# Expert loop by pairs: where half of one tile's second layer, the slot tables and a weight refill stand

## The chip, the cores and the metric

The kernel runs on one core of a Trainium2 chip. The metric is the device time of one execution in microseconds (us); the time before is the median of three runs. The engines are TensorE (PE, with its weight loads as PEld), VectorE (DVE), ScalarE (ACT), GpSimd (POOL) and SyncE (SP, which here only starts transfers). Each works through a queue of its own in order, and waits on semaphores that the other engines count up.

## What is computed

A chunked attention (8 batches, 8 heads, 576 positions, chunks of 64) gives x, 4608 tokens of 512 numbers. Then a layer of 8 experts: each token gets one expert, by the largest of 8 router logits or, where a local gate is open, the expert of the token before it.

```
for b, s:
    fresh_e = argmax(x[b, s] @ w_gate)
    e = fresh_e if s == 0 or local_gate[b, s] < 0.5 else prev_e
    p = softmax(x[b, s] @ w_gate)
    out[b, s] = p[e] * (relu(x[b, s] @ w1[e]) @ w2[e])     # w1: 512 x 1024, w2: 1024 x 512
```

## The kernel before

**Stages.** Attention goes in 18 blocks of 256 tokens until about 174 us. Tokens are then sorted by expert into tiles of 128 slots, an expert's share rounded up to 64, so that a tile may hold the end of one expert and the beginning of the next (a mixed tile). Tiles 0 to 2 (`EARLY` = 3) always belong to expert 0 and come from the first half of the tokens; their two layers run in the drain of the attention, in an order written out by hand (`PAR["drain"]`: `x2` is tile 2's transposes and split, `m2` its layer 1, `h2` the transposes of h, `y2` the four quarters of its layer 2 and its output, `x3` and `x4` the same of tiles 3 and 4 as `x2`, `ex` steps of the table of experts, `sl` steps of a table of slots). From tile 3 on a loop takes two tiles at a time (`two`, sixteen pairs, a = 3, 5, ... 33), and the last tiles go one by one (`step`).

**Precision.** fp32 products are made of three passes with the operands split into a high and a low half: high x high, high x low, low x high. The high half is a cast on ACT, the low half a subtraction on DVE. That holds for x (`XP`), h (`HP`), and both weights (`w1h`, `w1l`, `w2h`, `w2l`, four chunks each).

**A pair.** In a uniform pair, where both tiles have one expert, layer 1 gives h already transposed, in eight blocks of 128 features, 256 tokens wide: 12 matmuls each (L992), two blocks to one PSUM bank of `TR` (three banks), which ACT and DVE then empty into h's halves, tile by tile (L999, L1000). Otherwise each tile has a layer 1 of its own (`up`, L684), and h is transposed afterwards (L650). `two(a)` runs: layer 1 for blocks 0 to 3; the rejoining of a mixed x; refill of w1 if tile a is the last of its expert; layer 2 of tile a-1 (`down`, L705, 24 matmuls of 512 columns in four quarters; not for the first pair); refill of w2 if tile a-1 was the last of its expert; three register loads for the next pair; layer 1 for blocks 4 to 7; transposes of the next two x tiles into `TR[1]` and `TR[2]` (`next_x`); the second refill of w1; layer 2 of tile a; the second refill of w2.

**Refill.** `refill(which, t)` stands under a conditional on a register that says whether tile t+1 has another expert. ACT casts four chunks of the loaded weights to the high half (`refill_hi`, L942), DVE subtracts four low halves (`refill_lo`, L948), and SP starts the load of the expert after that. An engine passes the conditional by a register load (L927), a compare-and-branch (L958) and a semaphore event, also where nothing is refilled; whoever reads the weights waits for that event. With `between` the refill of w2 is split: two chunks, then other work, then two chunks.

**Tables.** `slots` makes the gather and scatter indices. For tiles 9 and on it has four steps, `sl[0]` and `sl[1]` (one half of the tokens each, all on DVE, L597 to L601), `sl[2]` (36 matmuls) and `sl[3]`. The loop runs `sl[0:2]` after the first pair and `sl[2:4]` after the second.

**Tiles of this input.** Tile 5 is the last of expert 0, 8, 16, 19, 24, 25 and 32 those of the experts after it; 8, 19 and 32 are mixed. So tiles 5 and 6, 7 and 8, 19 and 20, 25 and 26, 31 and 32 are pairs without one expert, and the pairs that begin at tiles 9, 17, 25 and 33 refill w2 between their halves. Data of a few more names: `HB` and `MB` are the PSUM banks of `up` and of the mixed part, `YB` the two banks of layer 2's results, `hsb` h before its transposes.

Of the kernel before, what the change touches and what calls it, by code (L numbers as in the profile page):

```python
# [8 lines left out]
F32 = mybir.dt.float32  # L9
# [4 lines left out]
AF = mybir.ActivationFunctionType  # L14
# [40 lines left out]
    ),  # L55
    "p0": "AVPA",
    "p1": "PPPP",
# [11 lines left out]
def tile_attention_then_moe(ctx: ExitStack, tc, q, k, v, wg, wl, w1, w2, out):  # L69
# [432 lines left out]
    def run(fns):  # L502
        for fn in fns:
            fn()
# [218 lines left out]
    def new_y():  # L723
        return ps_o.tile([P, C], F32, name="y", tag="o")
# [31 lines left out]
    def x_atoms(t, ps=None):  # L756
        return hilo_atoms(lambda n: xgs[t][:, P * n:P * n + P], *x_of(t), ps)

    def h_of(t, g):
        return [HP[t % 3][g][:, a] for a in range(2)]  # L760

    def h_atoms(t, g, ps=None):
        return hilo_atoms(lambda n: hsb[:, 512 * g + P * n:512 * g + P * n + P], *h_of(t, g), ps)
# [32 lines left out]
        return atoms  # L796

    def early_m2(t):
        y = new_y()
        return [lambda c=c: mm2(0, y, c) for c in range(4)] + [lambda: emit_y(t, y, prc[t])]  # L800

# [154 lines left out]
    def refill(which, t, between=None):  # L956
        if between is None:
            with tc.If(reg(0, t, 1, [ET.Activation, ET.DVE, ET.SP]) != 0):  # L958
                refill_hi(which)
                refill_lo(which, t)  # L960
            return
        with tc.If(reg(0, t, 1, [ET.Activation]) != 0):
            refill_hi(which)
        with tc.If(reg(0, t, 1, [ET.DVE, ET.SP]) != 0):
            refill_lo(which, t, (0, 1))
        between()
        with tc.If(reg(0, t, 1, [ET.DVE, ET.SP]) != 0):
            refill_lo(which, t, (2, 3))
# [16 lines left out]
               lambda: (mm1_lower(pairx[:, 0], HB), mm1_upper(fullx, MB), relu_mixed(hsb, HB, MB)))  # L985

    def up_pair(a, f0):
        for f in range(f0, f0 + 4):
            hb = TR[f // 2 % 3]
            for c in range(4):  # L990
                for n, (x, w) in enumerate(PASSES):
                    nc.tensor.matmul(hb[:, 256 * (f % 2):256 * (f % 2) + 256], W1[w][c][:, P * f:P * f + P],  # L992
                                     XP[:, x, c].rearrange("p s t -> p (s t)"),
                                     start=(c == 0 and n == 0), stop=(c == 3 and n == 2))
            if f % 2:
                for n in range(2):
                    ps = hb.rearrange("p (f s t) -> p f s t", f=2, s=2)[:, :, n]
                    hi, lo = (z[:, f % 4 - 1:f % 4 + 1] for z in h_of(a + n, f // 4))
                    nc.scalar.activation(hi, ps, AF.Relu)  # L999
                    V.scalar_tensor_tensor(lo, ps, 0.0, hi.bitcast(F32), ALU.max, ALU.subtract)  # L1000

    def down(t, cs=range(4), shared=False):
        y, pr = YB[:, t % 2], prc[t]
        ysb = pc.tile([P, C], F32, name="ysb") if cs[-1] == 3 else None

        def plain():
            for c in cs:
                mm2(t, y, c)
            if cs[-1] == 3 and shared:
                V.tensor_scalar(ysb[:, 0:256], y[:, 0:256], pr, None, ALU.mult)  # L1010
                nc.scalar.mul(ysb[:, 256:C], y[:, 256:C], pr)
            elif cs[-1] == 3:
                V.tensor_scalar(ysb, y, pr, None, ALU.mult)  # L1013

        def both():
            for c in cs:
                mm2_lower([pair01[:, g] for g in range(2)], y, c)
            if cs[-1] == 3:
                mm2_upper(full01, MB)
                y_mixed(ysb, y, MB, pr)  # L1020

        either(mix[t], plain, both)
        if cs[-1] == 3:
            scatter(t, ysb)
# [19 lines left out]
    def two(a, uni):  # L1044
        pr = get_prob(a)
        run(pr[:2])
        with tc.If(nc.snap(uni, engines=list(MAN)) != 0) as cmp:
            up_pair(a, 0)
        with cmp.Else():
            up(a)  # L1050
        rejoin_x(a + 1)
        refill(0, a)
        run(pr[2:])
        if a > EARLY:
            down(a - 1)
        refill(1, a - 1)
        more = uniform(a + 2) if a + 2 in PAIRS else mix_of(a + 2)
        pr = get_prob(a + 1)
        run(pr[:2])

        def next_x():
            for n in range(1 + (a + 2 in PAIRS)):
                run(x_atoms(a + 2 + n, TR[1 + n]))

        with tc.If(uni != 0) as cmp:
            up_pair(a, 4)
            next_x()
        with cmp.Else():
            for g in range(2):
                run(h_atoms(a, g, TR[g]))  # L1070
            rejoin_h(a)
            up(a + 1)
            next_x()
            for g in range(2):
                run(h_atoms(a + 1, g, (TR[0], MB)[g]))
        rejoin_x(a + 2)
        refill(0, a + 1)
        run(pr[2:])
        down(a)
        refill(1, a)  # L1080
        rejoin_h(a + 1)
        return more
# [47 lines left out]
    def valid(t):  # L1130
        return reg(2, t, 1, [ET.PE, ET.Activation, ET.DVE, ET.Pool, ET.SP]) if t >= TMIN else None

    mix, ok = {}, {t: None for t in range(TMIN)}
    oks, mixs = {}, {}
    with tc.manual_schedule(engines=MAN | {ET.SP, ET.Pool}):
        HP += [[pa2.tile([P, 2, 4, P], F32R, name=f"hq{n}", tag=tag, bufs=bufs) for n, (tag, bufs) in enumerate(two_of)]
               for two_of in ((("xs", 3), ("xs", 3)), (("xs", 3), ("pT", 2)))]
        pairx = pc.tile([P, 1, 4, P], F32R, name="pairx", bufs=1)
        pair01 = pa2.tile([P, 2, 4, P], F32R, name="pair0", tag="xT", bufs=1)
        fullx, *full01 = [pc.tile([P, 4, HT], F32, name=f"full{n}", bufs=1) for n in "x01"]  # L1140
        TR += [trp() for _ in range(3)]
        HB = new_h()
        MB = ps_l.tile([P, 512], F32, name="m", tag="lg")
        YB = ps_o.tile([P, 2, C], F32, name="y", tag="o")
        for t in (EARLY + 2, EARLY + 3):
            gather_full(t)
        uni = uniform(EARLY)
        rejoin_x(EARLY)
        refill(0, EARLY - 1)
        for a in PAIRS:  # L1150
            uni = two(a, uni)
            if 19 <= a < 24:
                for t in (a + 17, a + 18):
                    oks[t] = valid(t)
                    mixs[t] = mixed(t)
            n = a - EARLY
            run(sl[n:n + 2])
            if a + 5 <= TMIN:
                for t in (a + 4, a + 5):
                    gather_full(t)  # L1160
            if a in (TMIN // 2 - 1, TMIN - 3):
                nc.gpsimd.drain()
        ok[TMIN] = oks[TMIN]
        for t in range(PAIRS[-1] + 2, TMIN + 3):
            step(t)
        with when(ok[TMIN + 2]):
            for t in range(TMIN + 3, NTILE + 1):
                step(t)
# [21 lines left out]
```

## Time and profile before

| | us |
|---|---|
| median of 3 runs | 673.73 (671.21 to 676.15) |
| the profiled execution | 672.63 |
| its span, first to last instruction | 670.8 |
| PE busy | 624.3 (93%) |
| DVE busy | 380.4 (57%) |
| ACT busy | 259.9 (39%) |
| POOL busy | 151.7 (23%) |
| mean granted PE clock | 0.987 of full speed |

The span is cut in 40 slices for the busy shares; PE's digit is 8 or 9 in all but the first and the last slice. The chain that ended last names PE for 1% of the span and little else, so it does not help here; the waits of PE and the timeline do. A row of the timeline gives start, duration, engine, line, operation, output<-inputs, shapes and count, and in brackets how long the engine was idle before it and what released it. A name such as DVEq L958 means an instruction of that engine's sequencer (a wait or a branch). Durations of matmuls are those of a pipeline, so the distance of starts tells their rate.

### The profile page before, as it was taken

How to read it: one execution, taken by the hardware profiler on the slowest of the kernel's cores; microseconds unless marked ns; L12 is line 12 of the kernel's file. 1: busy time of each engine (PE TensorE's matmuls, PEld its weight loads, DVE VectorE, ACT ScalarE, POOL GpSimd, SP SyncE). 2: the span in 40 equal slices, each digit the busy share in tenths (PEclk: the TensorE clock that was granted, in tenths of full speed). 3: DMA queues.
4: the chain of work that ended last, by engine and by line, in shares of the span. 5: the costliest groups of instructions: out<-in, count | busy, mean ns of one | idle time of the engine just before them, and what ended most of it. 6: DMA issues, size and time to landing. Idle time of an engine off the chain costs nothing. (4 is left out here: it accounts for less than half of the span.)

```text
span 670.8 us, 17087 instructions
## 1 busy us (share of the span) xinstructions
PE 624.3 (93%) x5904; PEld 520.8 (78%) x5904; DVE 380.4 (57%) x983; ACT 259.9 (39%) x469; POOL 151.7 (23%) x209
## 2 busy tenths in 40 slices
PE   4799998889998989999999999999998999999995
PEld 4678776767787868777989887788986988788883
DVE  2666766887785576476334365664377533377231
ACT  4577765665312144342112342532266121243120
POOL 4433333460051121111212022020211311111201
PEclk9999998898999999999999999999999999999998
DMA  9999999978622053254211155422257510154101
GB/s 249 263 253 282 263 276 273 240 212 256 208 72 105 22 172 106 87 174 141 67 50 38 47 175 170 159 85 103 66 177 268 183 52 34 49 176 141 67 20 36
DMA packets 102515, 97.57 MB, mean 145 GB/s; under 512 B 42256, under 2 KB 79120, under 8 KB 102352
## 3 DMA queue, kind: packets, MB, share of 16 engines
q1 hardware_dynamic: 96192, 75.69, 38.1%
q0 software_dynamic: 6160, 19.85, 9.0%
q8 instruction: 85, 1.39, 0.9%
q14 instruction: 78, 0.64, 0.3%
HBM read 76.48 MB, written 19.56 MB: 143 GB/s over the span
## 5 line engine op out<-in xcount | busy, mean ns | idle before, releaser
L992 PE MATMUL tr<-xp,w1h 128*128 128x256 f32 x704 | 130.9, 283 | 1.9 <-ACTq L958 1.7
L766 POOL DMA_INDIRECT out<-ysb,sidx x38 | 44.3, 1166 | 372.0 <-DVEq L958 219.9
L992 PEld LDWEIGHTS tr<-xp,w1h 128*128 128x128 f32 x704 | 111.0, 191 | 4.4 <-ACTq L958 1.9
L705 PE MATMUL y<-w2h,hq 128*128 128x512 f32 x320 | 105.3, 399 | 1.0 <-ACTq L980 1.0
L992 PE MATMUL tr<-xp,w1l 128*128 128x256 f32 x352 | 100.4, 285 | 2.8 <-DVE w1l L948 2.2
L705 PE MATMUL y<-w2h,hp 128*128 128x512 f32 x240 | 78.6, 396 | 0.6 <-ACT hp L652 0.3
L705 PEld LDWEIGHTS y<-w2h,hq 128*128 128x128 f32 x320 | 60.4, 189 | 15.0 <-issue 1.2
L992 PEld LDWEIGHTS tr<-xp,w1l 128*128 128x128 f32 x352 | 67.2, 191 | 5.2 <-DVE w1l L948 3.5
L705 PE MATMUL y<-w2l,hq 128*128 128x512 f32 x160 | 63.5, 397 | 0.0
L684 PE MATMUL h<-w1h,xp 128*128 128x512 f32 x208 | 60.7, 397 | 0.0
L999 ACT ACTIVATE hq<-tr 128x256 fp32r<-128x256 f32 x48 | 18.4, 384 | 104.3 <-PE tr L992 73.8
L705 PEld LDWEIGHTS y<-w2h,hp 128*128 128x128 f32 x240 | 44.9, 188 | 11.6 <-issue 1.4
L705 PE MATMUL y<-w2l,hp 128*128 128x512 f32 x120 | 46.8, 390 | 0.0
L1013 DVE TENSOR_SCALAR ysb<-y,ppr 128x512 f32<-128x512 f32 x31 | 23.3, 751 | 40.0 <-PE y L705 39.5
L656 POOL DMA_INDIRECT xg<-x_d,gidx x36 | 39.8, 1105 | 18.9 <-issue 8.5
L684 PEld LDWEIGHTS h<-w1h,xp 128*128 128x128 f32 x208 | 37.9, 188 | 7.3
L999 ACT ACTIVATE hp<-tr 128x256 fp32r<-128x256 f32 x40 | 15.3, 383 | 71.7 <-PE tr L992 60.2
L653 DVE TENSOR_TENSOR xp<-tr,xp 128x512 fp32r<-128x512 f32 x39 | 25.6, 687 | 24.5 <-ACT xp L652 17.9
L1000 DVE SCALAR_TENSOR_TENSOR hq<-tr,hq 128x256 fp32r<-128x256 f32 x48 | 20.4, 424 | 32.9 <-ACT hq L999 28.6
L751 ACT ACTIVATE hsb<-h 128x512 f32<-128x512 f32 x26 | 14.1, 596 | 63.8 <-PE h L684 49.6
L948 DVE TENSOR_TENSOR w1l<-raw,w1h 128x1024 fp32r<-128x1024 f32 x28 | 32.4, 1220 | 8.6 <-ACT w1h L942 4.2
L251 PE MATMUL o<-v,pT 64*64 64x65 f32 x1152 | 27.8, 227 | 8.7 <-DMA v<-in_v 4.2
(219 smaller groups left out, 1110.2 us busy)
## 6 DMA issues: line engine op xcount, KB each, us to landing
raw<-in_moe_w SPq DMA_DIRECT2D x72, 512.0 KB, 4.1
x_d<-xs SPq DMA_DIRECT2D x16, 521.0 KB, 5.7
v<-in_v SPq DMA_DIRECT2D x32, 256.0 KB, 6.6
qt<-in_q SPq DMA_DIRECT2D x15, 512.0 KB, 6.9
kt<-in_k SPq DMA_DIRECT2D x15, 512.0 KB, 5.8
x_d<-xs SPq DMA_DIRECT2D x8, 130.2 KB, 4.8
qt<-in_q SPq DMA_DIRECT2D x8, 128.0 KB
kt<-in_k SPq DMA_DIRECT2D x8, 128.0 KB, 4.4
```

The costliest lines, as they stand in the source:

```text
L251: nc.tensor.matmul(o[64 * cp:64 * cp + 64, cc, DV * h:DV * h + D + 1], pT[64 * cc:64 * cc + 64, 4 * j + h, 64 * cp:64 * cp + 64], vt[64 * ...
L653: lambda: V.tensor_tensor(lo, box["ps"], hi.bitcast(F32), ALU.subtract)]
L656: nc.gpsimd.indirect_dma_start(out=dst, out_offset=None, in_=src, in_offset=bass.IndirectOffsetOnAxis(ap=gidx[t].bitcast(U32), axis=0))
L684: nc.tensor.matmul(hs[:, j], xs[a][:, c], W1[w][c][:, 512 * j:512 * j + 512], start=(c == 0 and n == 0), stop=(c == 3 and n == 2))
L705: nc.tensor.matmul(y, h_of(t, f // 4)[a][:, f % 4], W2[w][c][:, f % 2, :], start=(f == 0 and n == 0), stop=(f == 7 and n == 2))
L751: nc.scalar.activation(hsb[:, 512 * j:512 * j + 512], hs[:, j], AF.Relu)
L766: nc.gpsimd.indirect_dma_start(out=out, out_offset=bass.IndirectOffsetOnAxis(ap=sidx[t].bitcast(U32), axis=0), in_=ysb, in_offset=None, bo ...
L948: V.tensor_tensor(lo[c], raw[c], hi[c].bitcast(F32), ALU.subtract)
L992: nc.tensor.matmul(hb[:, 256 * (f % 2):256 * (f % 2) + 256], W1[w][c][:, P * f:P * f + P], XP[:, x, c].rearrange("p s t -> p (s t)"), star ...
L999: nc.scalar.activation(hi, ps, AF.Relu)
L1000: V.scalar_tensor_tensor(lo, ps, 0.0, hi.bitcast(F32), ALU.max, ALU.subtract)
L1013: V.tensor_scalar(ysb, y, pr, None, ALU.mult)
```

## The change

Tile 2's layer 2 is cut: two quarters stay in the drain, the other two and the output come between the halves of the first pair's layer 1, where the later pairs have the layer 2 of the tile before. For this tile 2 writes into `YB`, which is made earlier, and h's buffers rotate by one so that tile 2 keeps its own. The first half of the table for tiles 9 and on moves from behind the first pair to a place in its middle, ahead of that layer 2. In a uniform pair's layer 1 two blocks now go together: first all passes with `w1h` (16 matmuls), then those with `w1l` (8). The second half of a pair stands between two halves of w2's refill, so that DVE and SP pass one more conditional in each pair; the register loads for the next pair come ahead of it. The next x tiles are transposed into `TR[1]` and `MB` in a uniform pair, into `TR[2]` and `TR[1]` otherwise.

```diff
-  "... x3 p2 l1 x3 ex*2 l1 sl y2*2 x4*3 y2*2 "
+  "... x3 p2 l1 x3 ex*2 l1 sl y2 x4*3 "

     def h_of(t, g):
-        return [HP[t % 3][g][:, a] for a in range(2)]
+        return [HP[(t + 1) % 3 if t >= EARLY else 0][g][:, a] for a in range(2)]

     def early_m2(t):
+        if t == EARLY - 1:
+            late["y"] = ps_o.tile([P, 2, C], F32, name="y", tag="o")
+            return [lambda c=c: mm2(0, late["y"][:, t % 2], c) for c in range(2)]
         y = new_y()

     def up_pair(a, f0):
-        for f in range(f0, f0 + 4):
+        for f in (f0, f0 + 2):
             hb = TR[f // 2 % 3]
-            for c in range(4):
-                for n, (x, w) in enumerate(PASSES):
-                    nc.tensor.matmul(hb[:, 256 * (f % 2):256 * (f % 2) + 256], W1[w][c][:, P * f:P * f + P],
-                                     XP[:, x, c].rearrange("p s t -> p (s t)"),
-                                     start=(c == 0 and n == 0), stop=(c == 3 and n == 2))
-            if f % 2:
-                ...
+            for w, xs in ((0, (0, 1)), (1, (0,))):
                 for n in range(2):
+                    for c in range(4):
+                        for x in xs:
+                            nc.tensor.matmul(hb[:, 256 * n:256 * n + 256], W1[w][c][:, P * (f + n):P * (f + n) + P],
+                                             XP[:, x, c].rearrange("p s t -> p (s t)"),
+                                             start=(w + n + c + x == 0), stop=(w == 1 and n == 1 and c == 3))
+            for n in range(2):
+                ...

     def two(a, uni):
         ...
-        if a > EARLY:
-            down(a - 1)
-        refill(1, a - 1)
+        if a == EARLY:
+            run(sl[0:1])
+        down(a - 1, range(4) if a > EARLY else (2, 3))
         more = uniform(a + 2) if a + 2 in PAIRS else mix_of(a + 2)
         pr = get_prob(a + 1)
-        run(pr[:2])
-        def next_x():
-            for n in range(1 + (a + 2 in PAIRS)):
-                run(x_atoms(a + 2 + n, TR[1 + n]))
-        with tc.If(uni != 0) as cmp:
-            up_pair(a, 4)
-            next_x()
-        with cmp.Else():
-            ...
+        def next_x(*banks):
+            for n, ps in enumerate(banks[:1 + (a + 2 in PAIRS)]):
+                run(x_atoms(a + 2 + n, ps))
+        def second():
+            run(pr[:2])
+            with tc.If(uni != 0) as cmp:
+                up_pair(a, 4)
+                next_x(TR[1], MB)
+            with cmp.Else():
+                for g in range(2):
+                    run(h_atoms(a, g, TR[g]))
+                rejoin_h(a)
+                up(a + 1)
+                next_x(TR[2], TR[1])
+                for g in range(2):
+                    run(h_atoms(a + 1, g, (TR[0], MB)[g]))
+        refill(1, a - 1, second)
         rejoin_x(a + 2)

-    mix, ok = {}, {t: None for t in range(TMIN)}
+    mix, ok = {EARLY - 1: None}, {t: None for t in range(TMIN)}
-        YB = ps_o.tile([P, 2, C], F32, name="y", tag="o")
+        YB = late["y"]
-            n = a - EARLY
-            run(sl[n:n + 2])
+            if a == EARLY:
+                run(sl[1:2])
+            elif a == EARLY + 2:
+                run(sl[2:4])
```

## Rows read from the trace of the kernel before

**Rows 1.** The page's part 1: busy time, share and instructions.
```profile
PE 624.3 (93%) x5904; PEld 520.8 (78%) x5904; DVE 380.4 (57%) x983; ACT 259.9 (39%) x469; POOL 151.7 (23%) x209
```

**Rows 2.** Windows: length, busy us (count) of PE, PEld, DVE, ACT, POOL; PEclk, DMA, GB/s.
```profile
320.00:400.00 80.00, 79.30 (x505) 71.54 (x505) 32.90 (x91) 20.89 (x48) 13.39 (x14) 1.00 0.25 78
252.00:254.00 2.00, 2.00 (x10) 1.90 (x9) 1.68 (x3) 1.46 (x3) 0.00 (x0) 0.50 0.05 12
```

**Rows 3.** Waits of PE, whole span: us in total, times, longest.
```profile
PE tr L650 <- DVEq L932: 6.1, 2, 3.1
...
PE tr L992 <- DVE w1l L948: 2.2, 6, 0.5
```

**Rows 4.** Timeline of PE and DVE where the drain ends and the first pair begins.
```profile
207.32 0.60 PE L650 MATMUL tr<-ident,xg 128*128 128x128 f32 x4
207.81 0.17 DVE L637 TENSOR_TENSOR sidx<-gidx,pad 128x6 int32<-128x6 int32 x1
208.58 0.69 DVE L653 TENSOR_TENSOR xp<-tr,xp 128x512 fp32r<-128x512 f32 x1 [0.60 <-ACT xp L652]
209.14 0.28 PE L992 MATMUL tr<-xp,w1h 128*128 128x256 f32 x1
```

**Rows 5.** Timeline of PE and DVE, second half of the first pair.
```profile
216.76 0.39 PE L992 MATMUL tr<-xp,w1h 128*128 128x256 f32 x1 [1.66 <-ACTq L958]
217.70 0.39 PE L992 MATMUL tr<-xp,w1l 128*128 128x256 f32 x1 [0.56 <-DVEq L958]
217.73 0.17 DVE L671 TENSOR_TENSOR pex<-pex,ehot 128x8 f32<-128x8 f32 x1 [0.88 <-DVEq L958]
221.34 0.42 DVE L1000 SCALAR_TENSOR_TENSOR hp<-tr,hp 128x256 fp32r<-128x256 f32 x1 [0.24 <-ACT hp L999]
223.44 1.04 PE L650 MATMUL tr<-ident,xg 128*128 128x128 f32 x8
```

**Rows 6.** Groups of DVE from 231.3 to 238.65, both table halves: busy, mean ns.
```profile
L601 DVE TENSOR_TENSOR qv<-qeq,iota_t 128x666 bf16<-128x666 bf16 x4 | 3.4, 847 | 0.0
L597 DVE TENSOR_TENSOR qeq<-qs,iota_h 128x666 bf16<-128x666 f32 x4 | 3.2, 848 | 0.6 <-DVEq L932 0.6
L600 DVE TENSOR_SCALAR qv<-qeq,pcol 128x666 bf16<-128x666 bf16 x4 | 1.6, 390 | 0.0
```

**Rows 7.** Timeline, tiles 5 and 6 (248 to 255) and tiles 25 and 26.
```profile
248.98 1.29 DVE L653 TENSOR_TENSOR hq<-tr,hq 128x512 fp32r<-128x512 f32 x2
250.33 1.58 PE L650 MATMUL tr<-ident,xg 128*128 128x128 f32 x8 [2.93 <-DVEq L932]
...
254.24 0.63 PE L705 MATMUL y<-w2h,hq 128*128 128x512 f32 x2
...
511.84 1.09 PE L650 MATMUL tr<-ident,xg 128*128 128x128 f32 x8 [3.14 <-DVEq L932]
...
514.12 0.63 PE L705 MATMUL y<-w2h,hq 128*128 128x512 f32 x2
```

**Rows 8.** Timeline of PE, the pair of tiles 9 and 10, its first matmuls.
```profile
290.89 0.38 PE L992 MATMUL tr<-xp,w1l 128*128 128x256 f32 x1 [0.52 <-DVE w1l L948]
```

**Rows 9.** Timeline of DVE and PE, the same pair's second half.
```profile
304.60 4.63 DVE L948 TENSOR_TENSOR w2l<-raw,w2h 128x1024 fp32r<-128x1024 f32 x4
309.60 0.42 DVE L1000 SCALAR_TENSOR_TENSOR hp<-tr,hp 128x256 fp32r<-128x256 f32 x1
310.95 0.66 PE L650 MATMUL tr<-ident,xg 128*128 128x128 f32 x4 [1.52 <-DVE hq L1000]
```

**Rows 10.** Timeline, a pair without refill (27, 28), layer 2 of tile 27.
```profile
537.17 0.47 PE L705 MATMUL y<-w2h,hp 128*128 128x512 f32 x1
538.34 1.29 DVE L653 TENSOR_TENSOR xp<-tr,xp 128x512 fp32r<-128x512 f32 x2
540.24 0.39 PE L705 MATMUL y<-w2l,hp 128*128 128x512 f32 x1
```

**Rows 11.** Register loads of line 927 on DVE's queue: count, ns min/median/max.
```profile
L927 DVEq TENSOR_LOAD <-regs x138: 297/304/569, 198.9 to 665.8; - x138
```

More of the change, by code (lines that the diff above doesn't have):

```diff
@@ L987, in up_pair @@
     def up_pair(a, f0):
-        for f in range(f0, f0 + 4):
+        for f in (f0, f0 + 2):
             hb = TR[f // 2 % 3]
-            for c in range(4):
-                for n, (x, w) in enumerate(PASSES):
-                    nc.tensor.matmul(hb[:, 256 * (f % 2):256 * (f % 2) + 256], W1[w][c][:, P * f:P * f + P],
-                                     XP[:, x, c].rearrange("p s t -> p (s t)"),
-                                     start=(c == 0 and n == 0), stop=(c == 3 and n == 2))
-            if f % 2:
-                for n in range(2):
[L997 to L1000, printed above, removed]
+            for w, xs in ((0, (0, 1)), (1, (0,))):
+                for n in range(2):
+                    for c in range(4):
[4 more added lines that the diff above has]
+            for n in range(2):
+                ps = hb.rearrange("p (f s t) -> p f s t", f=2, s=2)[:, :, n]
+                hi, lo = (z[:, f % 4:f % 4 + 2] for z in h_of(a + n, f // 4))
+                nc.scalar.activation(hi, ps, AF.Relu)
+                V.scalar_tensor_tensor(lo, ps, 0.0, hi.bitcast(F32), ALU.max, ALU.subtract)
     def down(t, cs=range(4), shared=False):
@@ L1053, in two @@
         run(pr[2:])
-        if a > EARLY:
-            down(a - 1)
-        refill(1, a - 1)
+        if a == EARLY:
+            run(sl[0:1])
+        down(a - 1, range(4) if a > EARLY else (2, 3))
         more = uniform(a + 2) if a + 2 in PAIRS else mix_of(a + 2)
         pr = get_prob(a + 1)
-        run(pr[:2])
-        def next_x():
-            for n in range(1 + (a + 2 in PAIRS)):
-                run(x_atoms(a + 2 + n, TR[1 + n]))
-        with tc.If(uni != 0) as cmp:
-            up_pair(a, 4)
-            next_x()
-        with cmp.Else():
[L1069 to L1075, printed above, removed]
+        def next_x(*banks):
[15 more added lines that the diff above has]
+        refill(1, a - 1, second)
         rejoin_x(a + 2)
```

2 rows, old and new, of the table PAR are left out of this document.

## The prediction

> **What bounds the kernel now.** Times are us from the span's start. TensorE (PE) is busy for 93% of the span [rows 1], and in the expert loop, from 209 on, for nearly all of it: 79.30 of 80.00 between 320 and 400 [rows 2]. So I read only PE's own holes there; what VectorE (DVE) or ScalarE (ACT) saves counts when it ends one of them. The table of PE's waits names the large ones [rows 3], and the timeline places them. There are five kinds, and I price each by starts: the first late matmul against the start that an unbroken row would give (one matmul of 512 columns each 0.229, of 256 each 0.12).
>
> First pair: between its halves PE waits for ACT and then DVE to pass the conditional of the first layer's refill, which is not even taken, 1.66 and 0.56 idle [rows 5], 2.63 by starts. Second pair (tiles 5, 6): 2.93 idle until DVE has split h [rows 7], and the matmuls behind it run at half clock (granted 0.50, 1.2 GHz, between 252 and 254 [rows 2]): from the transposes at 250.33 to the third matmul of layer 2 at 254.24 it takes 3.9, where the same work behind a like hole takes 2.3, 511.84 to 514.12 [rows 7]. With the hole, 3.1 by starts, that is 4.7 for this one place. Three pairs that begin with a new expert wait for w1l: six holes, 2.2 idle in all [rows 3], one shown [rows 8], 3.2 by starts. Two pairs wait before the second x transpose, 1.52 [rows 9] and 0.98, for DVE, which splits w2 first. Last, pair 25 waits 3.14 at 511.84 [rows 7]. The rest belongs to edges that the diff does not touch.
>
> **The change part by part.**
>
> *Half of tile 2's layer 2 moved.* Twelve matmuls leave the place behind tile 4's transposes and go between the first pair's halves; 12 x 0.229 = 2.74, the same in both places. Where they left they had covered tile 4's split: transposes at 207.32, ACT's copy, DVE's subtraction from 208.58 to 209.27, first pair at 209.14 [rows 4]. Six of the twelve stood ahead of the transposes, so these now start at 205.95 and the copy ends near 207.2; but DVE is still busy with the first table's indices until 207.98 [rows 4], so the subtraction ends at 208.7. The second matmul of the pair reads it in either order of the passes. The pair starts in effect at 208.6 rather than 209.14, with PE idle for some 2.2 before. Its first half ends at 214.4, the moved matmuls fill to 217.15, and by then ACT's conditional (216.7 before, now 0.5 earlier) is passed; DVE's is passed at about 217.1 (217.73 in [rows 5], less 0.5), and w1l is wanted only 16 matmuls = 1.9 later. So the hole of 2.63 goes, and 2.2 of it comes back ahead of the pair: the next x transposes start at 222.95 rather than 223.44 [rows 5], 0.5 gained.
>
> *Tables at another place.* One table half is five kinds of pass, 2 x 0.85 + 2 x 0.85 + 2 x 0.39, with overlaps 3.66 on DVE [rows 6]. It now stands in the first pair ahead of tile 2's scaling, the register loads, and everything that DVE does for the second half. DVE reached the first split of that half at 221.34 [rows 5]. Now: conditional passed 217.1, five small ops to 218.1, table to 221.8, scaling 0.75 with three loads and a conditional behind it, first split about 224.65. From the first split to the end of the second x subtraction the refilled pair took 309.60 [rows 9] to 313.44 = 3.84 (its last link is two subtractions of 1.29 together, as at 538.34 in [rows 10]); so 228.5 here. Behind that stands the new second w2 conditional, and layer 2 of tile 3, started at 223.75, wants the third quarter of w2l at its 14th matmul, 3.07 later (537.17 to 540.24 [rows 10]), at 226.8. That is a new hole of 1.8, part of it already at the first matmul that reads a low half of h. The first pair as a whole loses 1.8 - 0.5 = 1.3. In the second pair the other table half alone stays: DVE is free of it 3.66 earlier, starts w1l when ACT delivers it (0.7 of the 3.66 is lost to that), and the split of h, 248.98 to 250.3 before, ends 2.9 earlier, as PE ends the layer. The first x transpose moreover goes to a bank that nobody holds. I take the whole 4.7 as gained; below it is bounded by 1.5 (hole halved, no clock loss saved), above by 4.9.
>
> *High passes first.* Of a pair of blocks the 16 matmuls with w1h run first, so w1l chunk 3 is wanted at 19 x 0.12 = 2.3 after the start rather than at 1.2. At 288.5 + 2.3 = 290.8 DVE's fourth chunk would just be there (290.8). But the new conditional of w2 stands ahead of it. Two conditionals in a row held DVE for 0.88, one of them with a register load [rows 5], so one with a load costs 0.3 (if it runs beside work) to 0.88; I take 0.45, as its load can run while the last subtraction does. That leaves 0.5 of each 1.07: gain 3 x 0.54 = 1.6, between 0.3 and 3.2. A register load on DVE took 304 ns in the median [rows 11]. The Trainium skill ("DMA: Bandwidth & Descriptors", section "Latency and other measured facts") gives a floor of about 600 ns for a tensor_load; by it the conditional would cost 0.75 and this term fall to 0.7; the trace has half that, so I keep the rows.
>
> *Second x in the mixed bank, and w2's refill in two halves.* These belong together in the pairs that begin with a new expert. In the first (tiles 9, 10) DVE split four chunks, 304.60 to 309.15, before it came to h at 309.60, and PE's second x transpose waited for h [rows 9]. Now no x transpose waits, layer 2 starts 1.8 earlier. DVE first loads registers (they have moved ahead of the refill: three loads of 0.3 [rows 11] with their handling, some 1.4), splits two chunks by 308.4 and reaches h at 308.8 rather than 309.60; x is done at 312.6, and only then the third chunk is split, to 313.9. PE wants it at 309.63 + 3.07 = 312.7: a new hole of 1.2. Net 0.6. For the second such pair the same sum gives 1.3 - 0.8 = 0.5, for the fourth, which had hardly waited, a loss of 0.2. Pair 25 has layer 1 of two single tiles: its x transpose into the free bank runs at once, the second waits for h, split 0.6 earlier, so 0.9 of the 3.14 come back. Sum 1.8, from 0 (the new hole eats all) to 4.5 (the last chunks run early enough).
>
> *The conditional once more in all sixteen pairs.* Where nothing is refilled, it stands behind the x subtractions, which end at 538.34 + 1.29 = 539.63, and PE wants w2l at 540.24 [rows 10]: 0.6 for a load that can be issued ahead and a branch. I take nothing, and 0.3 a pair as the bad end. SP's extra conditional and the later issue of half of w2's loads have a tile or more until the next use. ACT has as many conditionals as before.
>
> Sum: -1.3 + 4.7 + 1.6 + 1.8 = 6.8. The profiled execution took 672.63 (span 670.8 and 1.8 around it), so 665.8 by it. It lies 1.1 under the median of the runs, 673.73; against that median I forecast **667.0**.
>
> **The rivals.** (a) *The second pair's hole stays*, because its releaser there is the conditional of rejoining h and DVE's chain behind the table half is longer than I have it. For it: DVE still carries a table half there. Against it: 2.9 of slack by my sum for 2.93 needed. Then 6.8 - 4.7 = 2.1 gained, 671.6. (b) *The first pair's new hole does not come*, as layer 2's wait is met by an earlier count than the second conditional's. For it: waits here are counts on one semaphore of an engine; against: PE did wait at 216.76 and 217.70 for untaken conditionals. Then 8.6 gained, 665.1. (c) *The clock falls in the new hole ahead of the first pair.* It fell behind the hole of 2.93 and not behind the one of 3.14 [rows 2, 7]; the new one is 2.2. Price 1.6: 668.6. The Trainium skill ("TensorE: Matmul & The Clock Gate", Part 1) says that the throttled state is the default and that activity releases it, which speaks against opening holes at all; the two rows show that a hole of this size may or may not cost it. (d) *Slower:* the second w2 conditional ends late in every pair. Its place is the 14th matmul of layer 2, its margin 0.6. If DVE passes it d after the margin, 16 pairs cost 16 d; from d = 0.43 on, that is if it takes 1.0 behind the subtractions, the 6.8 are gone, and at the 0.88 + 0.6 of three conditionals passed one after the other d is near 0.9 and the time 673.7 - 6.8 + 14 = 681. Against it: the order in the code puts it first of the three.
>
> **How the numbers follow.** The sum holds with 0.55, (a) 0.15, (b) 0.15, (c) 0.1, (d) 0.05. Range: low end 673.73 - 8.6 and 2.3 more where the refilled pairs reach their good end, 662.8; high end (a) with a little of (d), 672.0. A measurement of this kernel tells about 1% = 6.7 from no change, so the forecast sits on the bound: of the sum's 0.55 half is faster by more, with (b) nearly whole: 0.43 faster; the other half, (a) and most of (c): 0.52 within; (d): 0.05 slower.
>
> **What would show it.** Right: no hole near 216 but one of 2 at 206 to 209; a hole of 1 to 2 in tile 3's layer 2 on DVE; none before the x transposes of tiles 7 and 8, and full clock there; w1l waits of 0.5, three of them; in the pairs of 9 and 17 a hole in the middle of layer 2 in place of the one before x. Wrong: DVE holes in layer 2 of pairs without a refill, or the second pair's hole unchanged.

## The result and the profile after

The median of 17 runs is 666.41 us (663.44 to 671.33) beside 674.84 (671.21 to 677.05) of the kernel before in 17 runs: a ratio of 0.9883, 95% interval 0.9861 to 0.9906. The forecast was 667.0, in a range of 662.8 to 672.0. The profiled execution has a span of 664.5.

The waits of PE after, over the whole span (total, times, longest), the rows that answer to [rows 3]:

```profile
PE tr L650 <- DVEq L935: 2.1, 1, 2.1
...
PE y L705 <- DVE w2l L951: 1.9, 3, 1.0
PE tr L997 <- DVE w1l L951: 1.4, 3, 0.7
...
PE y L705 <- DVEq L970: 0.3, 1, 0.3
```

The wait on h's split fell from 6.1 in two to 2.1 in one, that on w1l from six to three; three waits on w2l are new, and a small one on the second w2 conditional (L970). A hole below is a place where PE stands idle, a split DVE's subtraction that makes a low half. The timeline after of PE and DVE from the first pair's start to its layer 2 places the holes, beside [rows 4, 5]:

```profile
208.14 0.39 PE L997 MATMUL tr<-xp,w1h 128*128 128x256 f32 x1 [0.68 <-ACT xp L652]
209.55 2.06 PE L997 MATMUL tr<-xp,w1h 128*128 128x256 f32 x15 [1.02 <-DVE xp L653]
...
218.04 2.08 PE L997 MATMUL tr<-xp,w1h 128*128 128x256 f32 x16
...
221.84 0.84 DVE L601 TENSOR_TENSOR qv<-qeq,iota_t 128x666 bf16<-128x666 bf16 x1
222.60 0.74 DVE L1017 TENSOR_SCALAR ysb<-y,ppr 128x512 f32<-128x512 f32 x1
223.89 0.42 DVE L1004 SCALAR_TENSOR_TENSOR hq<-tr,hq 128x256 fp32r<-128x256 f32 x1
...
228.17 0.50 PE L705 MATMUL y<-w2l,hq 128*128 128x512 f32 x1 [0.31 <-DVEq L970]
```

No bracket stands behind 218.04: the hole between the halves is gone, and one of 2.12 by starts stands ahead of the pair. In tile 3's layer 2 only 0.48 is lost, as the first split comes 1.2 behind the end of the table (222.68). Then the second pair and a window of its layer 2 (columns as in [rows 2]), which answer to [rows 2, 7]:

```profile
247.03 1.29 DVE L653 TENSOR_TENSOR hp<-tr,hp 128x512 fp32r<-128x512 f32 x2
...
248.25 1.03 PE L650 MATMUL tr<-ident,xg 128*128 128x128 f32 x8
...
250.05 0.48 PE L705 MATMUL y<-w2h,hp 128*128 128x512 f32 x1
```

```profile
252.00:254.00 2.00, 2.00 (x10) 1.66 (x9) 0.75 (x2) 1.54 (x2) 0.00 (x0) 1.00 0.00 0
```

No hole, and the granted clock is 1.00 where it was 0.50. Last the pair of tiles 9 and 10, beside [rows 8, 9], and pair 25's hole, beside [rows 7]:

```profile
288.06 0.86 PE L997 MATMUL tr<-xp,w1l 128*128 128x256 f32 x5 [0.75 <-DVE w1l L951]
...
310.01 0.50 PE L705 MATMUL y<-w2l,hq 128*128 128x512 f32 x1 [1.00 <-DVE w2l L951]
...
505.27 0.66 PE L650 MATMUL tr<-ident,xg 128*128 128x128 f32 x4 [2.12 <-DVEq L935]
```

The hole ahead of the x transposes (1.68 by starts at 310.95 before) is replaced by one of 1.16 in the middle of layer 2.

**A finer measure than the time.** Single runs of this kernel differ by several us, most parts of the change by less. But every trace shows when tile 0's layer 2 starts and when that of the last tile does, tile 37 (the expectations call it tile 36); the attention lies ahead. These are the two rows of the kernel before and the two of after:

```profile
181.17 0.50 PE L705 MATMUL y<-w2h,hp 128*128 128x512 f32 x1
...
657.91 0.47 PE L705 MATMUL y<-w2h,hq 128*128 128x512 f32 x1 [0.96 <-ACTq L980]
```

```profile
182.10 0.50 PE L705 MATMUL y<-w2h,hp 128*128 128x512 f32 x1
...
650.74 0.47 PE L705 MATMUL y<-w2h,hq 128*128 128x512 f32 x1 [1.13 <-DVEq L967]
```

The stretch between them went from 476.74 to 468.64, 8.1 less. Over all the traces below, the first of the two starts lies anywhere from 172.25 to 182.10, though all edits lie behind it; from there on two traces agree tile by tile, mostly within 0.05 and at worst by about 0.1, where they run the same program, but for the clock; that one source can come out as two programs shows below. So parts are compared by this stretch, and by the distance from one tile's layer 2 to the next. "Less falls" takes off what half clock cost, read as the loss at that tile beyond the change of its hole. It is an estimate: where PE alone was slowed, a hole that PE would have met a little later can be hidden (drain_back).

| kernel | median us | ratio to before (95%) | stretch | falls of the clock | less falls |
|---|---|---|---|---|---|
| before | 674.84 | | 476.74 | 1 | 474.9 |
| after | 666.41 | 0.9883 (0.9861 to 0.9906) | 468.64 | 0 | 468.6 |
| after_again | 663.17 | 0.9885 (0.9854 to 0.9915) | 470.84 | 1 | 469.3 |
| tables_back | 665.61 | 0.9866 (0.9830 to 0.9902) | 472.28 | 1 | 471.0 |
| drain_back | 663.58 | 0.9833 (0.9797 to 0.9869) | 469.77 | 1 | 468.1 |
| passes_back | 668.15 | 0.9885 (0.9850 to 0.9919) | 473.09 | 1 | 471.7 |
| unsplit | 667.77 | 0.9870 (0.9834 to 0.9907) | 473.63 | 2 | 468.6 |
| bank_back | 664.71 | 0.9897 (0.9832 to 0.9963) | 473.43 | 2 | 470.3 |
| high_alone | 666.94 | 0.9937 (0.9900 to 0.9974) | 474.45 | 2 | 471.0 |
| drain_x4 | 661.74 | 0.9840 (0.9765 to 0.9916) | 469.82 | 1 | 468.3 |
| lo_first | 664.73 | 0.9892 (0.9856 to 0.9928) | 473.09 | 1 | 471.6 |
| table_early | 657.88 | 0.9791 (0.9755 to 0.9828) | 467.81 | 1 | 466.4 |
| loads_behind | 661.27 | 0.9869 (0.9830 to 0.9910) | 469.18 | 0 | 469.2 |
| combo | 656.58 | 0.9782 (0.9754 to 0.9810) | 465.31 | 0 | 465.3 |

The kernels ran in three sets, in each beside the kernel before: tables_back to unsplit (its median there 674.96), bank_back to lo_first (671.65), and the last three with after_again (671.67). So a median is read by its ratio.

### The profile page after: what moved, and what is told of

The parts are those of the page before. It is cut to its first block, busy times and chain, and to the rows that moved or that the text cites. A ratio compares the mean times of both kernels' runs of the same rounds, so it can differ in the third digit from the quotient of the medians.

```text
span 664.5 us, 17370 instructions
## 1 busy us (share of the span) xinstructions
PE 624.6 (94%) x5904; PEld 521.3 (78%) x5904; DVE 378.2 (57%) x983; ACT 259.1 (39%) x469; POOL 146.8 (22%) x209
## 5 line engine op out<-in xcount | busy, mean ns | idle before, releaser
L705 PE MATMUL y<-w2h,hq 128*128 128x512 f32 x368 | 120.7, 398 | 1.1 <-DVEq L967 1.1
L997 PE MATMUL tr<-xp,w1h 128*128 128x256 f32 x704 | 92.1, 283 | 2.0 <-DVE xp L653 1.0
L997 PEld LDWEIGHTS tr<-xp,w1h 128*128 128x128 f32 x704 | 88.7, 191 | 5.2 <-ACT w2h L945 1.5
L705 PE MATMUL y<-w2l,hq 128*128 128x512 f32 x184 | 73.1, 397 | 1.7 <-DVE w2l L951 1.3
L705 PE MATMUL y<-w2h,hp 128*128 128x512 f32 x192 | 62.8, 395 | 0.5 <-ACT hp L652 0.3
L997 PE MATMUL tr<-xp,w1l 128*128 128x256 f32 x352 | 50.2, 284 | 1.4 <-DVE w1l L951 1.4
L997 PEld LDWEIGHTS tr<-xp,w1l 128*128 128x128 f32 x352 | 45.6, 192 | 2.0 <-DVE w1l L951 2.0
L705 PEld LDWEIGHTS y<-w2l,hq 128*128 128x128 f32 x184 | 34.6, 188 | 10.5 <-DVE w2l L951 2.5
L705 PE MATMUL y<-w2l,hp 128*128 128x512 f32 x96 | 37.6, 392 | 0.5 <-DVE w2l L951 0.5
L951 DVE TENSOR_TENSOR w2l<-raw,w2h 128x1024 fp32r<-128x1024 f32 x28 | 32.9, 1220 | 5.7 <-issue 2.4
```

Source lines behind the costliest of these rows:

```text
L705: nc.tensor.matmul(y, h_of(t, f // 4)[a][:, f % 4], W2[w][c][:, f % 2, :], start=(f == 0 and n == 0), stop=(f == 7 and n == 2))
L951: V.tensor_tensor(lo[c], raw[c], hi[c].bitcast(F32), ALU.subtract)
L997: nc.tensor.matmul(hb[:, 256 * n:256 * n + 256], W1[w][c][:, P * (f + n):P * (f + n) + P], XP[:, x, c].rearrange("p s t -> p (s t)"), star ...
```

## The experiments

**after_again**: the changed kernel with no edit.

> The changed kernel once more, nothing edited. Theory (the spread of the times lies ahead of the loop, in the attention and its scatter, and in the clock; the loop repeats itself): tile 0's layer 2 begins anywhere between 176 and 183, and from there to tile 36's the stretch is 468.6 again within 0.3, plus 1.3 to 1.9 for each stretch of half clock in it; no hole before the loop's clock falls differs by more than 0.1. Rival (the loop itself varies with the transfers of x and the weights): its holes differ by 0.5 or more.

Tile 0's layer 2 began at 173.60. The stretch was 470.84, of it 1.55 half clock behind the hole of pair 25. But the hole ahead of the first pair was 2.93 and not 2.12 by starts, the hole in pair 9's layer 2 was 0.86 and not 1.16, pair 33's w1l wait 0.97 and not 0.57. The theory's 0.1 fell, and holes differ by 0.8, as the rival had it, but the place points to the queues and not to transfers. It is another program: the same source came out with its register loads in other places. The register loads of line 930 (count, ns min/median/max, first and last start), of after and then of this run:

```profile
L930 DVEq TENSOR_LOAD <-regs x154: 297/306/553, 199.8 to 658.8; - x154
...
L930 PEldq FUSED_REGOPS  x39: 146/151/162, 204.2 to 598.0; - x39
...
L930 DVEq FUSED_REGOPS  x16: 183/183/209, 201.2 to 571.9; - x16
```

```profile
L930 DVEq TENSOR_LOAD <-regs x154: 297/306/543, 197.1 to 652.3; - x154
...
L930 PEldq FUSED_REGOPS  x55: 146/146/163, 195.7 to 591.8; - x55
```

PE passes 55 register operations instead of 39, and the 16 of DVE's queue are gone from there. DVE's first loads run 23.5 behind tile 0's layer 2 instead of 17.7: close ahead of tile 4's subtraction instead of well before it, where DVE idles 0.99 for them instead of 0.16, the 0.8 of the first hole. In pair 9 DVE idles 1.33 ahead of the first chunk of w2l instead of 1.63, the 0.30 by which that hole is shorter. The chip is not the reason: tables_back and unsplit repeat this run's holes, drain_back and passes_back those of after, and all four ran on one chip. All traces below but two repeat this run's holes where their code is the same, and are compared with it; those of drain_back and passes_back repeat the 1.16 of after and are compared with that, and high_alone with before.

**tables_back**: both table halves behind the first pair.

```diff
-        if a == EARLY:
-            run(sl[0:1])
...
-                run(sl[1:2])
+                run(sl[0:2])
```

> Everything of the change is kept but the place of the tables: both halves run after the first pair again. Theory (the table half on DVE made the second pair late): the second pair's x transposes stop after the first tile's four and wait about 2.6 us for DVE's split of h (248.3 before, now 3.7 less 0.7 later), the half clock may come back behind it (1.6), and the first pair's hole of 0.48 at 228 goes; time 668.7 without the clock's fall, 670.3 with it. Rival (the first x transpose's other bank, or the register loads' new place, is what freed the second pair): no hole over 0.5 there, time 666 as with the whole change.

The timeline of the second pair, and windows at the first pair's start and in the second pair's layer 2:

```profile
247.97 1.29 DVE L653 TENSOR_TENSOR hp<-tr,hp 128x512 fp32r<-128x512 f32 x2
249.31 0.66 PE L650 MATMUL tr<-ident,xg 128*128 128x128 f32 x4 [2.17 <-DVEq L935]
```

```profile
207.00:210.00 3.00, 2.85 (x13) 2.85 (x14) 0.09 (x1) 0.00 (x0) 0.00 (x0) 0.50 0.01 3
249.50:253.00 3.50, 3.50 (x22) 3.06 (x22) 2.58 (x4) 2.28 (x5) 0.00 (x0) 1.00 0.07 22
```

The second pair's hole is back, 2.32 by starts, where 2.6 was expected, and the first pair's 0.5 is gone: the theory holds, 1.7 in the stretch less falls. The clock fell at another place than expected, in the first pair. The time, 665.61, would have pointed to the rival, but a loss of 1.7 is 0.25% of it and its interval is 0.72% wide: the time can't tell, the stretch can.

**drain_back**: tile 2's whole layer 2 in the drain.

```diff
-... ex*2 l1 sl y2 x4*3
+... ex*2 l1 sl y2*2 x4*3 y2*2
...
-        down(a - 1, range(4) if a > EARLY else (2, 3))
+        if a > EARLY:
+            down(a - 1)
```

> Tile 2's whole layer 2 is back in the drain, all else of the change is kept. Theory (the moved half only trades one hole for another, and what is left hangs on DVE's chain): the hole of 2.1 ahead of the first pair shrinks to under 0.7, PE waits 1.9 to 2.6 for ACT's conditional between the first pair's halves, and tile 3's layer 2 waits about 1.4 instead of 0.48; sum +0.6, time 667.0. Rival (the cover between the halves is worth the whole hole of 2.6): time 669.

PE between the first pair's halves, and a window behind it:

```profile
213.42 2.91 PE L998 MATMUL tr<-xp,w1h 128*128 128x256 f32 x13 [1.95 <-ACTq L962]
```

```profile
214.00:216.50 2.50, 2.50 (x13) 2.50 (x13) 2.26 (x8) 0.00 (x0) 0.00 (x0) 0.50 0.00 0
```

DVE's first split behind the table:

```profile
219.27 0.42 DVE L1005 SCALAR_TENSOR_TENSOR hq<-tr,hq 128x256 fp32r<-128x256 f32 x1
```

The hole ahead of the pair is gone, one of 2.10 stands between the halves instead: the move trades one for the other, as the theory had it. But tile 3's layer 2 then lost nothing instead of 1.4. The clock hides that hole: counted from tile 0's layer 2 (here at 177.45), this split starts as late as in after (41.82 beside 41.79), while half clock makes tile 3's layer 2 start 1.63 later (44.11 beside 42.48), more than the 0.48 that it lost there. So the 0.5 by which the stretch, less falls, is shorter than after is no gain of this edit: the part is worth about nothing, and a run without the fall is missing.

**passes_back**: the three passes of each chunk together.

```diff
-            for w, xs in ((0, (0, 1)), (1, (0,))):
-                for n in range(2):
-                    for c in range(4):
-                        for x in xs:
+            for n in range(2):
+                for c in range(4):
+                    for p, (x, w) in enumerate(PASSES):
```

> The three passes of each chunk stand together again, all else of the change is kept. Theory (high passes first give 1 us at each of the three pairs that begin with a new w1): the w1l holes at 288, 386 and 589 go from 0.98, 0.37, 0.57 to 1.9, 1.3, 1.5, sum +2.8, time 669.2. Rival (the order only moves the wait, the fourth chunk decides either way): +0.5 or less, 666.9.

PE at the start of the pair of tiles 9 and 10:

```profile
285.42 0.39 PE L996 MATMUL tr<-xp,w1l 128*128 128x256 f32 x1 [0.35 <-DVE w1l L951]
...
286.56 0.38 PE L996 MATMUL tr<-xp,w1l 128*128 128x256 f32 x1 [0.51 <-DVE w1l L951]
...
287.69 0.38 PE L996 MATMUL tr<-xp,w1l 128*128 128x256 f32 x1 [0.52 <-DVE w1l L951]
```

Three waits instead of one, 1.86 by starts (1.9 expected); each of the three refilled pairs lost 1.07 to 1.09, 3.2 in all. The theory holds.

**high_alone**: the kernel before with the changed order of the passes alone, as the change has it in `up_pair`.

> The kernel before with nothing changed but the order of the passes. Theory (the extra conditional takes back part of this step's gain; without it the fourth chunk is just in time): the six w1l waits vanish, 3.2 by starts, and the wait for DVE's conditional in the first pair (0.82) too; the stretch from tile 0's to tile 36's layer 2 goes from 476.74 to 472.7. Rival (about 0.5 is left of each wait whatever stands ahead): 474.3.

No w1l wait is left, nor the one on DVE's conditional in the first pair; the three pairs gained 1.07, 1.09 and 1.08, the first 0.69. Less falls 471.0 beside 474.9: 3.9, where the theory had 4.0. So this step alone ends these waits, and in the changed kernel something takes part of that back. DVE's first chunk of w1l for tiles 9 and 17, before and then after:

```profile
286.20 1.23 DVE L948 TENSOR_TENSOR w1l<-raw,w1h 128x1024 fp32r<-128x1024 f32 x1 [0.72 <-DVEq L932]
...
385.30 1.23 DVE L948 TENSOR_TENSOR w1l<-raw,w1h 128x1024 fp32r<-128x1024 f32 x1 [0.73 <-ACT w1h L942]
```

```profile
283.38 1.22 DVE L951 TENSOR_TENSOR w1l<-raw,w1h 128x1024 fp32r<-128x1024 f32 x1 [1.58 <-ACT w1h L945]
...
381.07 1.22 DVE L951 TENSOR_TENSOR w1l<-raw,w1h 128x1024 fp32r<-128x1024 f32 x1 [1.17 <-ACT w1h L945]
```

In brackets is DVE's idle time since the split before it: 0.86 and 0.44 more. Where the releaser named is a copy of w1h, that had ended before; what came last was the conditional on DVE's own queue. That the extra one is the reason, unsplit shows, which leaves it out.

**unsplit**: w2's refill whole again, ahead of the second half.

```diff
-        refill(1, a - 1, second)
+        refill(1, a - 1)
+        second()
```

> w2's refill stands whole ahead of the second half again, so the extra conditional is gone in all sixteen pairs; the other parts are kept, the mixed bank too. Theory (the bank alone frees the x transposes, the split is worth as much as its conditional costs): in the pairs of tiles 9, 17 and 33 the hole in the middle of layer 2 goes and one of about 1.6, 1.1 and 0.8 stands at its second matmul (+1.2), pair 25 waits 3.2 instead of 2.28 (+0.9), the w1l holes shrink to 0.1, 0 and 0.1 (-1.7), and the hole of 0.48 in the first pair goes; sum -0.1, time 666.3. Rival (the split is what gains in the refilled pairs, its conditional is nearly free): +1.8 or more, 668.2.

DVE's first chunk of w1l for tile 9, PE in the pairs of tiles 9 and 25, and a window behind the hole ahead of the first pair:

```profile
282.61 4.63 DVE L951 TENSOR_TENSOR w1l<-raw,w1h 128x1024 fp32r<-128x1024 f32 x4 [0.72 <-DVEq L935]
...
306.55 0.72 PE L705 MATMUL y<-w2h,hq 128*128 128x512 f32 x2 [0.87 <-DVE hq L1004]
...
505.53 0.69 PE L650 MATMUL tr<-ident,xg 128*128 128x128 f32 x2 [4.32 <-DVEq L935]
```

```profile
206.80:212.00 5.20, 4.45 (x21) 4.45 (x22) 0.69 (x2) 0.00 (x0) 0.00 (x0) 0.50 0.00 2
```

Ahead of w1l DVE idles 0.72 again, as in before, and no w1l wait is left. Less falls 468.6 beside 469.3: the split gains nothing in sum. It gains 2.2 in pair 25 and loses 0.6 or so at each of the first pair and the pairs of 9, 17 and 33, by its conditional. The two falls here cost 5.0 and hide that. The rival falls, and so does the size of the theory's parts (1.04 and not 1.6 in pair 9, 2.2 and not 0.9 in pair 25).

**bank_back**: x to TR[1] and TR[2] again.

```diff
-                next_x(TR[1], MB)
+                next_x(TR[1], TR[2])
...
-                next_x(TR[2], TR[1])
+                next_x(TR[1], TR[2])
```

> The next x tiles go to TR[1] and TR[2] in both kinds of pair again, all else of the change is kept. Counted from tile 0's first layer-2 matmul to tile 36's (476.74 before, 468.64 after), the stretch that the attention's own scatter does not touch. Theory (bank and split go together: with the split DVE reaches h so early that the old bank costs little): in the pairs of tiles 9 and 17 the second x transpose waits 1.1 and 0.5, the hole in the middle of layer 2 shrinks by half of it, pair 25 loses 0.5; sum +1.5. Rival (the bank alone is what gained 1.8 and 1.3 there): +3.1.

PE in the first pair and in that of tiles 9 and 10:

```profile
223.73 0.66 PE L650 MATMUL tr<-ident,xg 128*128 128x128 f32 x4 [0.87 <-DVE hq L1004]
...
305.07 0.66 PE L650 MATMUL tr<-ident,xg 128*128 128x128 f32 x4 [0.44 <-DVE hq L1004]
```

The wait ahead of x is back in pair 9, 0.59 by starts, and the whole hole behind it goes: the bank alone is worth nothing there. The sum is 1.0, nearly all of it in the first pair (0.5) and pair 25 (0.6); the theory's 1.5 is nearer than the rival's 3.1.

**drain_x4**: tile 4's x ahead of a table of scatter indices (the expectation has its tiles wrong, they are 3 to 8).

```diff
-... ex*2 l1 sl y2 x4*3
+... ex*2 l1 x4*2 y2 x4 sl
```

> The changed kernel, with tile 4's transposes, copy and subtraction ahead of the scatter indices of tiles 0 to 5 in the drain. Theory (the hole of 2.1 ahead of the first pair is only the order of DVE's queue): under 0.4 of it is left, the hole in tile 3's layer 2 grows by at most 0.5; the stretch goes from 468.64 to 466.8, and the clock can't fall there. Rival (DVE's chain in the first pair is the bound): the hole comes back between or behind the halves, 468.5.

PE at the first pair's start and in tile 3's layer 2:

```profile
205.65 0.62 PE L997 MATMUL tr<-xp,w1h 128*128 128x256 f32 x3 [0.65 <-DVEq L961]
...
225.31 0.50 PE L705 MATMUL y<-w2l,hq 128*128 128x512 f32 x1 [0.98 <-DVEq L970]
```

2.09 was gained ahead of the pair, with 0.81 of the hole left where under 0.4 was expected, and 1.00 given back in it, between theory and rival: PE comes earlier, DVE's chain through the table half not as much.

**lo_first**: the second half of w2l ahead of x on DVE, under a conditional inside each branch.

```diff
                 up_pair(a, 4)
+                lo_w2((2, 3))
                 next_x(TR[1], MB)
...
                     run(h_atoms(a + 1, g, (TR[0], MB)[g]))
+                lo_w2((2, 3))
...
+        def lo_w2(cs):
+            with tc.If(reg(0, a - 1, 1, [ET.DVE]) != 0):
+                for c in cs:
+                    V.tensor_tensor(w2l[c], raw2[c], w2h[c].bitcast(F32), ALU.subtract)
```

> The changed kernel, with the second conditional of w2's refill ahead of the next x tiles on DVE in uniform pairs (SP starts the loads in a conditional of its own behind). Theory (x is in no hurry, chunk 3 of w2l is): the holes in the middle of layer 2 (1.16, 0.67, 0.52) and the 0.48 of the first pair go, and w1l's holes lose about 0.4 each as the conditional runs while DVE waits for ACT's copy of x; sum -3.5, from 468.64 to 465.1. Rival (x becomes late and holds the next pair): the gain is lost again at the next pair's first matmuls, 468.6.

DVE and PE in the pair of tiles 9 and 10:

```profile
302.41 2.36 DVE L1087 TENSOR_TENSOR w2l<-raw,w2h 128x1024 fp32r<-128x1024 f32 x2 [0.43 <-issue]
304.69 0.68 DVE L653 TENSOR_TENSOR xp<-tr,xp 128x512 fp32r<-128x512 f32 x1
305.29 0.68 DVE L653 TENSOR_TENSOR xp<-m,xp 128x512 fp32r<-128x512 f32 x1
305.43 0.50 PE L705 MATMUL y<-w2l,hq 128*128 128x512 f32 x1 [1.57 <-DVE xp L653]
```

Theory and rival both fell. The chunks end at 304.77 and x holds nobody, but PE reads w2l only as the first x subtraction is done. The wait is one count on DVE's semaphore for both branches, and in the other branch the chunks come last; that this is why is argued from the order of the code and was not tried. It fits that PE is held two instructions too long in pair 9, where two x tiles follow, and only one, the second chunk, in pair 33, where one follows. Less falls it loses 2.3.

**loads_behind**: the register loads for the next pair behind the first half of w2's refill.

```diff
-        more = uniform(a + 2) if a + 2 in PAIRS else mix_of(a + 2)
...
         def second():
+            more.append(uniform(a + 2) if a + 2 in PAIRS else mix_of(a + 2))
```

> The changed kernel with the three register loads for the next pair back behind the first half of w2's refill. Theory (they held DVE for about 1.4 between the scaling and the first chunk of w2l, as the forecast had it): in the pairs of tiles 9, 17 and 33 the chunks start about 1 sooner and the holes in the middle of layer 2 (1.16, 0.67, 0.52) shrink to 0.2 or less; sum -2.0, stretch 466.6. Rival (DVE's chain there hangs on PE's own blocks and the x copies, not on the first chunks): the holes stay within 0.2, 468.6.

DVE and PE in the pair of tiles 9 and 10:

```profile
296.44 2.36 DVE L951 TENSOR_TENSOR w2l<-raw,w2h 128x1024 fp32r<-128x1024 f32 x2 [0.18 <-issue]
...
302.58 0.69 DVE L653 TENSOR_TENSOR xp<-tr,xp 128x512 fp32r<-128x512 f32 x1
...
305.10 0.50 PE L705 MATMUL y<-w2l,hq 128*128 128x512 f32 x1 [0.41 <-DVE w2l L951]
```

DVE waits 0.18 ahead of the first chunk instead of 1.33, so the loads did hold it for 1.15. Yet the hole in layer 2 only went from 0.86 to 0.58, and those of tiles 17 and 33 not at all: the last splits wait for PE's own blocks, as the rival had it. It gained 1.0 in pair 25 and lost 1.1 in the first pair.

**table_early**: drain_x4, and the table half ahead of the first pair's first split, where DVE stood idle for 3.53.

```diff
         refill(0, EARLY - 1)
+        run(sl[0:1])
         for a in PAIRS:
```

> The changed kernel with tile 4's x ahead of the scatter indices in the drain, and the first half of the table, from the middle of the first pair, to DVE's idle stretch ahead of that pair's first split. Theory (DVE's chain through the table half is what the first pair waits for): 0.8 or less left ahead of the first pair, no hole over 0.2 in tile 3's layer 2, tile 4's layer 2 begins 1.8 sooner after tile 0's than in the changed kernel; the stretch is 466.8 without a fall of the clock. Rival (the second w2 conditional ends that hole, wherever the table stands): 0.5 to 1.1 stays, 467.8.

PE at the first pair's start; behind it no hole follows until 280.86:

```profile
202.65 0.70 PE L997 MATMUL tr<-xp,w1h 128*128 128x256 f32 x2 [0.47 <-ACTq L961]
```

Tile 4's layer 2 comes 1.86 sooner after tile 0's than in after (1.8 expected), the stretch less falls is 466.4 (466.8): the theory holds.

**combo**: table_early and loads_behind together.

> The three edits together: tile 4's x first, the table half ahead of the first pair's splits, the register loads behind the first half of w2's refill. If both theories hold their gains add, as they lie in different pairs: stretch 464.8 without a fall of the clock, time 662.5 beside 666.4 of the changed kernel. If only the table's holds: 466.8; if neither, 468.6.

PE at the first pair's start and in pair 25, and a window behind the latter:

```profile
198.45 0.74 PE L997 MATMUL tr<-xp,w1h 128*128 128x256 f32 x4 [0.65 <-DVEq L961]
...
491.68 0.55 PE L650 MATMUL tr<-ident,xg 128*128 128x128 f32 x3 [1.17 <-DVEq L935]
```

```profile
492.00:495.00 3.00, 3.00 (x21) 2.64 (x19) 2.70 (x5) 1.92 (x5) 0.00 (x0) 1.00 0.85 330
```

The stretch is 465.3, the time 656.58 beside 663.17 of after_again on the same chip: the lowest median of all, at 0.9782 of before (its interval overlaps that of table_early). Of the 6.6 between these medians the stretches show 5.5, of which 1.55 is the fall in after_again. With the table out of the way the loads lose nothing in the first pair and still gain 1.0 in pair 25, whose hole of 1.32 by starts left the clock at 1.00.

## Why the prediction was right, and where not

Each step by the distance of layer 2 starts (its tiles in brackets) or, for the w1l waits, by their lengths, as a gain; after_again is less its fall:

| step | forecast | after | after_again |
|---|---|---|---|
| drain and first pair (0 to 4) | -1.3 | -0.1 | -1.0 |
| second pair (4 to 6) | 4.7 | 4.9 | 4.9 |
| high passes, three w1l waits | 1.6 | 1.3 | 0.9 |
| pair of 9 (8 to 10) | 0.6 | 0.6 | 0.9 |
| pair of 17 (16 to 18) | 0.5 | 0.6 | 0.6 |
| pair of 25 (24 to 26) | 0.9 | 0.8 | 0.8 |
| pair of 33 (32 to 34) | -0.2 | -0.3 | -0.3 |
| sum | 6.8 | 7.8 of 8.1 | 6.8 of 7.4 |

- **Half of tile 2's layer 2.** Right: 2.2 ahead of the pair was forecast, 2.12 came (2.93 in after_again), 0.5 at the x transposes, 0.57 came. drain_back adds that the move itself trades one hole for another.
- **The table half in the first pair**, the term that was mis-sized: a new hole of 1.8, measured 0.48. The chain of 3.84 from the first split to the end of x was 3.85 (223.89 to 227.74), the table ended where it was put (counted from tile 0's layer 2, which came 0.93 later in after); but the step from the table's end to the first split, put at 2.85 with a scaling, three loads and a conditional in a row, took 1.21. The scaling follows the table at once, and the loads, from 220.69 on, pass beside the table's last passes.
- **The second pair.** Right in size and cause: tables_back brings 2.32 of the hole back. Of its 4.9 the clock is 1.8, and 0.77 is left for x in a free bank (the hole of 3.09 less 2.32; not tried by itself with the tables back). The clock's part was counted as sure and is not: tables_back has the hole without the fall.
- **High passes.** Right: 3.2 alone, less what the extra conditional takes. It was put at 0.45 and measured 0.86, 0.44 and, at tile 33, 0.46, each DVE's idle time beyond that of before; in unsplit, without the conditional, nothing of it is left.
- **Bank and split.** Right in sum, each pair within 0.1 in after. Their shares were not separated in the forecast; unsplit and bank_back show that the split is worth nothing in sum, or a little less, and the bank 1.0, and that the split earns only in pair 25. Both taken back at once was not tried.
- **The conditional in all pairs.** Right: behind the first pair, no pair without a refill has a hole in layer 2, so rival (d) is out. Rival (a) did not come. Of (b) most came, the hole it left out being 0.48. Rival (c) did not come in after, but it did in tables_back, unsplit, bank_back and lo_first, at the same place behind a hole of 2.9; after_again and loads_behind have that hole without a fall.

The sum of 6.8 met a measured 8.4 between the medians, on a median that had itself come out 1.1 higher than the one shown before. That 667.0 lies so near 666.41 is therefore partly luck; the better check is the table, where in after one term of seven, the first pair, is off by 1.2 and no other by more than 0.3; in after_again the high passes are off by 0.7.

## What to carry to other kernels

Where the noise of the time is larger than a part of the change, find a stretch of the trace that repeats and compare starts inside it, tile by tile; and run the unedited kernel once more, since a new build may differ by as much as the edit (0.7 over the stretch here). A step that fills one hole of the bound engine is worth only what its removal does not open elsewhere, so ask first which engine's chain sets the end of the whole stretch (here DVE's through a table half), and put side work where that engine already idles.

## What the runs showed of the hardware

- **The clock behind holes.** In the 14 traces PE stood idle 23 times in the loop for 1.8 or more in one place (two waits with a few matmuls between them counted together). In or right behind 14 of them the granted clock fell to 0.50, 1.2 GHz, and at none of the shorter ones, the longest of which was 1.70 (after, ahead of the first pair). The same hole of pair 25 fell in after_again (2.17) and not in after (2.12). A fall cost 1.3 to 1.8, and 2.3 and 2.7 in unsplit. The Trainium skill ("TensorE: Matmul & The Clock Gate", Part 1) has the throttled state as the default that activity releases; the traces agree in that every fall in the loop stands at a hole, and show besides that such a hole brings one only part of the time: the longest without a fall was 3.14 (before, pair 25), the shortest with one 1.92 (passes_back, pair 25).
- **Conditionals.** One more that refills nothing held DVE for 0.44 to 0.86 (after beside before; unsplit, without it, has the idle time of before again); three register loads in a row for 1.15 where nothing covered them and for nothing that shows where passes of the table ran ahead of them.
